# Two first expert slots computed together, and a routing table read three units later

## The chip, the cores and the metric

The kernel runs on one core of one Trainium2 chip. The metric is device time in microseconds (us): the median of three runs of one program, from its first to its last instruction and what lies around that. A profile is one further execution, recorded instruction by instruction. PE is the matrix engine (TensorE), DVE the vector engine, ACT the scalar engine, POOL is GpSimd, SP is the engine that issues most DMAs; PEld is the weight load that belongs to a matmul.

## What is computed

Three layers in a row, all in float32: causal attention with a cumulative bias (4 batches, 8 heads, 576 positions, 64 wide), a mixture of 8 experts over the 2304 tokens that leave it, and a gated layer.

```python
def _moe_ref(x, modality_id, w_gate, modality_bias, w1, w2) -> np.ndarray:
    logits = x @ w_gate + modality_bias[modality_id]
    e_idx = np.argmax(logits, axis=1)
    ...
    gate_w = probs[np.arange(N), e_idx]
    for e in range(E):
        mask = e_idx == e
        h = np.maximum(x[mask] @ w1[e], 0.0)
        out[mask] = gate_w[mask, None] * (h @ w2[e])

def _moe2_ref(x, w_gate, w_val, w_out) -> np.ndarray:
    gate = 1.0 / (1.0 + np.exp(-(x @ w_gate)))
    val = x @ w_val
    return (gate * val @ w_out).astype(np.float32)
```

Every token goes to one expert, the one with the largest logit. Which tokens an expert has is known only while the kernel runs. The change touches the passage from attention to the experts.

## The kernel before

**Attention** (`Attention.run`) works through 16 pairs of heads in an order written out by hand. A batch is done after four pairs. `Router.batch` then appends that batch's routing steps to a queue `router.q`; `tick()` issues one step between two attention instructions, `pump(n)` issues n at once.

**Routing of a batch.** DVE reduces the logits, finds each token's expert and makes a one-hot matrix `oh`. Six small matmuls on PE (tile `rp`, the rank product) turn it into each token's place among the tokens of its expert. DVE makes the address `r_ix`; POOL then writes the token numbers into a table `tab` in device memory with five indirect DMAs ("scatters", `tab<-ids,r_ix`) of up to 128 numbers each, and SP writes the batch's tokens to `x` (`x<-xr`, `rows_out`: one DMA of 1026 KB and one of 128 KB).

**Early slots.** Experts work in slots of 256 tokens. After two of the four batches the kernel guesses the expert with the most tokens (`on_guess`, which loads its weights into the `raw` tiles) and fills slots 0 and 1 with tokens of it. These two (`EARLY = 2`) run while batches 2 and 3 are still being routed. Slots 2 to 8 come after the whole table is known.

**A unit.** A slot is worked off in 8 units, one for each 128 columns of the hidden layer: 12 matmuls of the first product (`mm1`, tile `ph`), then 12 of the second product of the unit before (`mm2`, into `sb` for even slots and `y` for odd ones). Between the two products ACT makes the rounded hidden tile `hH`, and DVE its remainder `hL`. The weights are split likewise (`split`): for each of the two weight pieces of a unit a rounded copy (ACT) and a remainder (DVE), tiles `ew` for the early slots and `w` later. The first three splits are made by POOL alone. Slots 0 and 1 have the same weights, and each makes its own splits: slot 0 takes units 0 to 7, slot 1 units 8 to 15. A slot's tokens are scaled (`gate`, tile `xg`), transposed on PE (`mtr`, four 128x128 blocks at a time, two times) and split into `xT` by ACT and DVE before its first unit.

**From the table to slot 2.** In `early`, `main(u)` pumps 14 routing steps after each unit: what is left of batch 3, then the 60-odd small DVE steps of `Router.slots` that compute which slot has which expert. In the middle of these POOL reads the table rows of all slots back (`fetch_rows`, `tid<-tab,row`); it waits for every scatter. `indices` transposes them on PE (`itr<-ident,tid`) and DVE makes the row numbers `idx`, with which POOL gathers slot 2's tokens. Then all engines load the register `more` (are there rare slots?), and SP loads slot 2's weights over the `raw` tiles. PE takes its instructions in order, so what stands behind `itr` waits with it.

A finished slot is copied to `yt` and stored to `x2`.

Of the kernel before, what the change touches and what calls it, by code (L numbers as in the profile page):

```python
# [8 lines left out]
F32 = mybir.dt.float32  # L9
# [488 lines left out]
BIG = 100000.0  # L498
TROWS, PUMP = 96, 14
GAP, SP = [1, 1, 0, 0], [6, 3, 6, 0]  # L500
EARLY, EARLYB, MAIN, SLOTS, FIRST = 2, 2, 9, 14, 3
MAINH, HALVES, HROW, NROW = 2, 8, 32, 40


class Router:
    def __init__(self, tc, cp, ap, ps, ident, mod_bias, mod_id, x, tab, B, S):
        self.tc, self.nc = tc, tc.nc
        nc = self.nc
# [45 lines left out]
        self.gap, self.apart_of = 1, {"tab": [], "y": [], "out": []}  # L554
        self.q, self.hold, self.side = [], False, None

# [51 lines left out]
    def batch(self, b, xr, lg):  # L608
# [5 lines left out]
        tile_ = lambda shape, nm, dt=F32: cp.tile(shape, dt, tag="r_" + nm, name="r_" + nm)  # L614
        st = {}
        self.q.append(lambda: setattr(self, "gap", GAP[b]))
        bc = lambda a: a.unsqueeze(2).to_broadcast([128, 5, 8])
# [7 lines left out]
        q = self.q  # L625
# [40 lines left out]
        q.append(lambda: V.tensor_scalar(se, se, 1e-9, None, ALU.add))  # L666
        q.append(lambda: V.reciprocal(xr[:, :, 512], se))
        for t in range(5):
            rows = 64 if t == 4 else 128
            self.space(SP[b])  # L670
            q.append(lambda t=t, rows=rows: self.apart("tab", nc.gpsimd.indirect_dma_start(
                out=self.tab.rearrange("r c -> (r c)").unsqueeze(1),
                out_offset=bass.IndirectOffsetOnAxis(ap=ix[:rows, t : t + 1], axis=0),
                in_=self.ids[:rows, b, t : t + 1], in_offset=None, bounds_check=TROWS * 256 - 1, oob_is_err=True)))
            if t > 2:
                q.append(lambda t=t: self.rows_out(b, t, xr))
        if b == EARLYB - 1:
# [22 lines left out]
            q.append(lambda: V.tensor_copy(self.guess_i, gf[0:1]))  # L700
            q.append(self.on_guess)

    def rows_out(self, b, t, xr):

        x = self.x[2 * self.S * (b // 2) : 2 * self.S * (b // 2 + 1), :].rearrange("(p j) r -> p j r", j=XS)
        if t == 4:
            dst, src = x[64 * (b % 2) : 64 * (b % 2) + 64, 8, :], xr[:64, 4, :]  # L710
        else:
            dst, src = x[:, 4 * (b % 2) : 4 * (b % 2) + 4, :], xr[:, 0:4, :]
        self.nc.sync.dma_start(dst, src)

    def fetch_rows(self, tid, row, n):
        self.behind("tab", self.nc.gpsimd.indirect_dma_start(
            out=tid[:n, :], out_offset=None, in_=self.tab[:, :],
            in_offset=bass.IndirectOffsetOnAxis(ap=row[:n, 0:1], axis=0), bounds_check=TROWS - 1, oob_is_err=True,
        ))

    def indices(self, nm, tid, n, last):
# [24 lines left out]
    def slots(self):  # L746
# [79 lines left out]
        op(V.scalar_tensor_tensor, out=more, in0=inc[0:1, 8:9], scalar=float(MAIN), in1=s0[0:1], op0=ALU.is_gt, op1=ALU.max)  # L826
        q.append(lambda: self.indices("idx", self.tid, NROW, self.B * self.S - 1))
        op(V.tensor_copy, rg[:, 2:3], base)
# [53 lines left out]
class Moe:  # L882
# [8 lines left out]
    def open(self, ctx, early):  # L891
        P = lambda n, c: c.enter_context(self.tc.tile_pool(name=n, bufs=1, side="right", reuse_waits="tile"))
        self.wk, self.pe = P("m_work", ctx), P("m_early", early)
        self.xg_t = [self.wk.tile([128, 2, RW], F32, name=f"xg{i}") for i in range(3)]
        self.yt = self.wk.tile([128, 4, 256], F32, name="yt")

# [118 lines left out]
    def store(self, s):  # L1015

        nc, n = self.nc, 128 if s >= HROW else 256
        del self.xg[s]
        y = self.y.pop(s)
        for c, p in enumerate(y):  # L1020
            nc.scalar.copy(self.yt[:, 4 // len(y) * c : 4 // len(y) * (c + 1), :n], p.rearrange("p (a t) -> p a t", t=n))
        at = 256 * s if s < EARLY else self.base(s)
        nc.sync.dma_start(self.x2.rearrange("(c p) t -> p c t", p=128)[:, :, bass.ds(at, n)], self.yt[:, :, :n])
        if s >= EARLY:
            self.place(s, at, n)
# [6 lines left out]

    def mm(self, s, f):
        h = self.mm1(s, f)
        if self.prev:
            self.mm2(*self.prev)
        self.prev = (s, f, h)
# [88 lines left out]

    LE, LA = 2, 3

# [12 lines left out]
    def first(self):  # L1141
        for s in range(EARLY):
            self.gather(s)
        for f in range(self.LE + 1):
            self.split(0, f, self.nc.gpsimd)
            if f == 0:
                self.gate(0)
        self.v, self.u = self.LE + 1, 0

    def look(self):  # L1150
        for h in range(2):
            self.transpose(0, h)

    def step(self, u):
        s, f = divmod(u, 8)
        self.mm(s, f)
        if f == 3 and s >= EARLY and s + 2 < MAIN + MAINH:
            self.gather(s + 2 if s + 2 < MAIN else s + 2 - MAIN + HROW)
        if f == 1 and s + 1 < MAIN and s + 1 != EARLY:
            self.gate(s + 1)  # L1160
        if f == 4 and s + 1 == EARLY:
            self.gate(EARLY, True)
        if f in (4, 5) and s + 1 < MAIN:
            self.transpose(s + 1, f - 4)

    def next(self):
        self.step(self.u)
        self.u += 1
# [6 lines left out]
    def early(self, main):  # L1175

        for u in range(8 * EARLY):
            if u == self.u:
                self.next()
            while not self.ready:  # L1180
                self.ready = main(u)
                if u < 8 * EARLY - 5:
                    break
            self.loads()
            for s in range(EARLY, EARLY + 2):
                if self.ready and s not in self.xg and u >= 8 * (EARLY - 2) + 13 * (s - EARLY):
                    self.gather(s)
            self.aheads(self.LE if self.v < 8 * EARLY else self.LA)

# [534 lines left out]
def kernel(ctx, tc, q, k, v, s, modality_id, moe_w_gate, modality_bias, w1, w2, wg, wv, wo, out):  # L1724
    nc = tc.nc
# [9 lines left out]
    with tc.manual_schedule():  # L1735
# [47 lines left out]
        def main(u):  # L1783
            if u >= 0:
                router.pump(PUMP)
            if not router.q and phase[0] == 0:
# [5 lines left out]
            if router.q or not phase[0]:  # L1792
                return False
            for s in range(EARLY):
                moe.place(s, 256 * s)
            more.append(nc.values_load(router.more[0:1, 0:1], min_val=0, max_val=1))
            return True
# [6 lines left out]
        def put(at, tasks):  # L1804
            todo.setdefault(at, []).extend(tasks)
# [5 lines left out]
        for k, stages in enumerate(glu.last_weight(pool(wo_ctx, "dec", side="right", reuse_waits="tile"))):  # L1811
            for i, task in enumerate(stages):
                put(2 * k + i - 55, [task])
        put(-28, [wo_ctx.close, open_xs, glu.dec.load, glu.dec.load])
        (d0, s0), (d1, s1) = glu.w_tasks(0, lambda: xs[0]), glu.w_tasks(1)
# [84 lines left out]
```

## Time and profile before

| | us |
|---|---|
| median of three runs | 946.76 (944.15 to 948.65) |
| profiled execution, its own time | 945.87 |
| its span, first to last instruction | 944.1 |
| PE busy in it | 899.6 (95%) |
| DVE, ACT, POOL busy | 710.0, 554.1, 397.2 |
| units 0 to 15 (the two early slots), start of the first to end of the last | 59.96 |

The kernel is bound by PE nearly everywhere. In the span's 40 slices PE is below 90% in four: the first, the last, and those from 283 to 307 us and from 519 to 543 us. The granted clock of PE is below 90% in the first and in the one from 283 to 307 us; the latter lies in the early slots. Rows give start and length in us from the span's start; a bracket at the end is the time that the engine sat idle before the row and what ended it.

### The profile page before, as it was taken

Reading aid. Unit: us, or ns where it says so; the run is one execution under the profiler, and the core shown is the slowest. Engines: PE = TensorE matmul, PEld = TensorE weight load, DVE = VectorE, ACT = ScalarE, POOL = GpSimd, SP = SyncE. Lnnn points to the kernel's source line nnn. Section 1 sums busy time; section 2 is a strip of 40 time slices with the busy share of each in tenths; the row PEclk is TensorE's granted clock in tenths of the full one; section 3 lists DMA queues with packets and bytes.
Section 4 is the critical chain, followed back from the end, with each engine's and each line's share of the span. In section 5 each row is a group of like instructions: output and inputs, shape, how many; then the busy total and the mean of one; then the engine's idle time right before and its main releaser. Section 6 shows DMA issues by size and latency. Waiting matters only on the chain. (4 is left out here: it accounts for less than half of the span.)

```text
span 944.1 us, 18712 instructions
## 1 busy us (share of the span) xinstructions
PE 899.6 (95%) x6261; PEld 861.0 (91%) x6261; DVE 710.0 (75%) x1583; ACT 554.1 (59%) x1296; POOL 397.2 (42%) x616
## 2 busy tenths in 40 slices
PE   7999999999997999999999899999999999999996
PEld 6899889888887999999998799999999999889996
DVE  6999999999894688867766667767575747878771
ACT  4999899898643665656544455454545344454440
POOL 7988789798742577776630001010000000111111
PEclk8999999999998999999999999999999999999999
DMA  7667559694382355723467322333232308473501
GB/s 173 157 155 161 135 87 128 165 125 145 139 102 69 95 174 180 280 90 90 137 225 242 99 79 95 112 101 120 70 132 76 126 11 296 137 242 111 168 35 44
DMA packets 163903, 125.34 MB, mean 133 GB/s; under 512 B 86737, under 2 KB 147692, under 8 KB 163286
## 3 DMA queue, kind: packets, MB, share of 16 engines
q1 hardware_dynamic: 158790, 113.62, 44.5%
q0 software_dynamic: 3792, 10.14, 3.2%
q8 instruction: 51, 0.84, 0.4%
q14 instruction: 54, 0.44, 0.2%
q10 hardware_dynamic: 1216, 0.30, 0.1%
HBM read 115.95 MB, written 33.23 MB: 158 GB/s over the span
## 5 line engine op out<-in xcount | busy, mean ns | idle before, releaser
L1342 PE MATMUL X<-a,set 128*128 128x384 f32 x864 | 164.7, 338 | 4.8 <-ACTq L1072 3.0
L1342 PEld LDWEIGHTS X<-a,set 128*128 128x128 f32 x864 | 152.4, 188 | 6.6 <-ACTq L1072 3.1
L861 POOL TENSOR_SCALAR dn<-dr 128x256 int8<-128x256 int8 (+1 forms) x60 | 35.2, 588 | 251.3 <-DMA dr<-in_moe_w_gate_dram 96.6
L925 POOL TENSOR_TENSOR w<-raw,w 128x512 fp32r<-128x512 f32 x56 | 79.6, 1431 | 57.2 <-ACT w L922 54.7
L174 POOL TENSOR_SCALAR bias<-cumB,cumT 128x576 f32<-128x576 f32 (+4 forms) x155 | 82.6, 535 | 25.7 <-DVE nm L293 21.3
L1479 POOL DMA_INDIRECT out_dram<-oy,row x18 | 20.0, 1113 | 169.2 <-ACT oy L1503 92.0
L989 PE MATMUL ph<-xT,w 128*128 128x256 f32 x672 | 90.0, 283 | 0.0
L989 PEld LDWEIGHTS ph<-xT,w 128*128 128x128 f32 x672 | 83.6, 188 | 0.0
L1342 PE MATMUL Y<-a,set 128*128 128x384 f32 x432 | 82.0, 338 | 0.0
L302 ACT ACTIVATE P<-P,nm 128x576 f32<-128x576 f32 (+3 forms) x128 | 79.5, 627 | 3.3 <-DVE nm L293 3.2
L337 DVE TENSOR_TENSOR PL<-pt,PH 128x512 fp32r<-128x512 f32 (+1 forms) x128 | 77.0, 629 | 1.9 <-ACT PH L330 1.4
L1342 PEld LDWEIGHTS Y<-a,set 128*128 128x128 f32 x432 | 76.5, 188 | 0.1
L1351 ACT COPY u<-X 128x384 f32<-128x384 f32 x72 | 34.5, 479 | 62.8 <-PE X L1342 62.7
L293 DVE CUSTOM_DVE_ANT_0 P<-sb,bias 128x320 f32<-128x320 f32 (+3 forms) x128 | 67.1, 548 | 2.4 <-PE sb L284 1.9
L330 ACT CAST PH<-pt 128x512 fp32r<-128x512 f32 (+1 forms) x128 | 64.8, 552 | 6.8 <-PE pt L321 5.2
L321 PE MATMUL pt<-ident,P 128*128 128x128 f32 x448 | 64.2, 277 | 3.1 <-DVE PL L337 1.2
L925 DVE TENSOR_TENSOR w<-raw,w 128x512 fp32r<-128x512 f32 x56 | 57.0, 1019 | 11.6 <-ACT w L922 10.8
L922 ACT CAST w<-raw 128x512 fp32r<-128x512 f32 x112 | 63.5, 619 | 0.0
L993 ACT ACTIVATE hH<-ph 128x256 fp32r<-128x256 f32 x72 | 27.7, 384 | 59.7 <-PE ph L989 59.5
L284 PE MATMUL sb<-KT,QH 128*128 128x288 f32 (+3 forms) x192 | 56.3, 317 | 6.6 <-DVE nm L293 4.7
L321 PEld LDWEIGHTS pt<-ident,P 128*128 128x128 f32 x448 | 50.6, 141 | 9.6 <-DVE PL L337 1.9
L1277 ACT CAST hf<-hp 128x768 fp32r<-128x768 f32 x42 | 34.1, 835 | 38.5 <-DVE hp L1279 35.4
(317 smaller groups left out, 2430.9 us busy)
## 6 DMA issues: line engine op xcount, KB each, us to landing
raw<-in_moe_w_dram SPq DMA_DIRECT2D x80, 512.0 KB
h<-sg SPq DMA_DIRECT2D x72, 192.0 KB
cumB<-cum_d SPq DMA_DIRECT2D x32, 288.0 KB
hp<-h SPq DMA_DIRECT2D x24, 384.0 KB
qraw<-in_q_dram SPq DMA_DIRECT2D x58, 128.0 KB
dr<-in_moe_w_out_dram SPq DMA_DIRECT2D x12, 511.6 KB
dr<-in_moe_w_gate_dram SPq DMA_DIRECT2D x24, 255.2 KB
dr<-in_moe_w_val_dram SPq DMA_DIRECT2D x24, 255.2 KB
```

The source lines that it names most:

```text
L174: (nc.vector if n in FILLB else nc.gpsimd).tensor_scalar(res[i][:rows], cumB[:rows, :m], -1.0, self.cumT[:rows, i, n : n + 1], ALU.mult, A ...
L284: nc.tensor.matmul(self.sb[:rows, o : o + c1 - c0], X[:, T0[i] : T0[i] + rows], h["KT"][:, c0:c1], start=j == 0, stop=j == 1)
L293: nc.vector.tensor_tensor_reduce(out=pt[:rows, :m], in0=self.sb[:rows, o : o + m], in1=self.bias_t[n][i][:rows], op0=ALU.add, op1=ALU.min, ...
L302: nc.scalar.activation(h["P"][i][:rows, : T0[i] + rows], h["P"][i][:rows, : T0[i] + rows], AF.Exp, bias=h["nm", i][:rows], scale=-1.0, acc ...
L321: nc.tensor.transpose(pt[:, c : c + 128], h["P"][i][:, T0[j] : T0[j] + 128], self.ident)
L330: self.nc.scalar.copy(t[:, :z], pt[:, :z])
L337: self.nc.vector.tensor_tensor(t[:, :z], pt[:, :z], h["H"][u][:, :z].bitcast(F32), ALU.subtract)
L861: nc.gpsimd.tensor_scalar(o["n"], top(), 56.0, -56.0, ALU.min, ALU.max)
L922: nc.scalar.copy(v, src)
L925: (eng or nc.vector).tensor_tensor(v, src, h.bitcast(F32), ALU.subtract)
L989: nc.tensor.matmul(ph, w[:, 128 * dc : 128 * dc + 128], x[:, dc], start=k == 0, stop=k == 11)
L1342: self.nc.tensor.matmul(bank, w[:, c], a[:, h, c], start=first and k == 0, stop=k == 5, skip_group_check=True)
```

## The change

Slots 0 and 1 are run alternately: unit u is column block u // 2 of slot u % 2, and the block is split once for both. Slot 1's tokens are scaled and transposed before its first unit, now unit 1; slot 2's are transposed inside units 14 and 15, between the first and the second product.

The steps of `main` are spread differently: 9 steps after unit 0, none after units 1 and 2, and 14 after each unit from 3 on. The product `itr` moves from behind unit 7 to behind unit 10. The last batch's token rows go out on POOL's queue after its five scatters, no longer on SP's ahead of them. `on_guess` moves from the end of batch 1's steps to the start of batch 2's, and batch 2's scatters are held back until POOL has its first two splits behind it. Slot 2's weights can be loaded once slot 0 has used a block. The register `more` is loaded behind unit 36. `yt` has two buffers.

```diff
-TROWS, PUMP = 96, 14
-GAP, SP = [1, 1, 0, 0], [6, 3, 6, 0]
-EARLY, EARLYB, MAIN, SLOTS, FIRST = 2, 2, 9, 14, 3
+TROWS, PUMPS = 96, (9, 0, 0, 14)
+GAP, SP = [1, 1, 0, 0], [6, 3, 0, 0]
+EARLY, EARLYB, MAIN, SLOTS, IDX = 2, 2, 9, 14, 10
...
+        if b == EARLYB:
+            self.q.append(self.on_guess)
...
+        if b == EARLYB:
+            q.append(lambda: setattr(self, "hold", not self.started))
...
-            if t > 2:
-                q.append(lambda t=t: self.rows_out(b, t, xr))
+            if t > 2 and b < self.B - 1:
+                q.append(lambda t=t: self.rows_out(b, t, xr, nc.sync))
+        if b == self.B - 1:
+            for t in (3, 4):
+                q.append(lambda t=t: self.rows_out(b, t, xr, nc.gpsimd))
...
+    def numbers(self):
+        self.indices("idx", self.tid, NROW, self.B * self.S - 1)
...
+        yt = self.wk.tile([128, 4, 256], F32, tag="yt", name="yt", bufs=2)
...
     def first(self):
         for s in range(EARLY):
             self.gather(s)
-        for f in range(self.LE + 1):
+        for f in range(2):
             self.split(0, f, self.nc.gpsimd)
             if f == 0:
-                self.gate(0)
-        self.v, self.u = self.LE + 1, 0
+                for s in range(EARLY):
+                    self.gate(s)
+        self.r.hold, self.r.started = False, True
+        self.e, self.u, self.v = 2, 0, 8 * EARLY
+        self.pend.append((EARLY, 0))
...
+    def both(self, u):
+        f, s = divmod(u, EARLY)
+        self.shared = self.piece[s, f] = self.shared if s else self.piece[s, f]
+        left = 8 * EARLY - u
+        self.mm(s, f, (lambda: self.transpose(EARLY, 2 - left)) if left < 3 else None)
+        if left == 4:
+            self.gate(EARLY, True)
...
     def early(self, main):
+        for h in range(2):
+            self.transpose(1, h)
         for u in range(8 * EARLY):
             if u == self.u:
                 self.next()
             while not self.ready:
                 self.ready = main(u)
-                if u < 8 * EARLY - 5:
+                if u < IDX:
                     break
+            if u == IDX:
+                self.r.numbers()
+                for s in range(EARLY):
+                    self.place(s, 256 * s)
+                self.gather(EARLY)
+            if u == 8 * EARLY - 3:
+                self.gather(EARLY + 1)
+            while self.e < min(8, u // EARLY + 3):
+                self.split(0, self.e)
+                if self.e % 2 == 1:
+                    self.pend.append((EARLY, self.e // 2))
+                self.e += 1
             self.loads()
...
-                router.pump(PUMP)
+                router.pump(PUMPS[min(u, 3)])
...
-            more.append(nc.values_load(router.more[0:1, 0:1], min_val=0, max_val=1))
...
+        put(-36, [lambda: more.append(nc.values_load(router.more[0:1, 0:1], min_val=0, max_val=1))])
```

On PE, behind unit 0: `trx` and `ptx` are the last attention products, `ph` the first product of unit 1, `mtr` the transposes. Before:

```order
L381 MATMUL trx<-wgx,oT 128x144 x3
L381 MATMUL ptx<-wgx,oT 128x144 x2
L989 MATMUL ph<-xT_5178,ew 128x256
L989 MATMUL ph<-xT_5179,ew 128x256
L989 MATMUL ph<-xT_5178,ew 128x256 x2
```

Now:

```order
L381 MATMUL trx<-wgx,oT 128x144 x3
L381 MATMUL ptx<-wgx,oT 128x144 x2
L980 MATMUL mtr<-ident,xg_5066 128x128 x8
L996 MATMUL ph<-xT_5261,ew 128x256
L996 MATMUL ph<-xT_5262,ew 128x256
L996 MATMUL ph<-xT_5261,ew 128x256 x2
```

Slot 1's eight transposes (`xg_5066`) now stand directly ahead of slot 1's first unit, with nothing between them.

On DVE, the last batch's way from its logits to the one-hot matrix `oh_193`, which the rank product reads. Before:

```order
L626 TENSOR_REDUCE r_L<-lg_195 128x40
L627 TENSOR_TENSOR r_L<-r_L,tb 128x40
L628 TENSOR_REDUCE r_mx<-r_L 128x5
L629 TENSOR_TENSOR r_eq<-r_L,r_mx 128x40
L630 SCALAR_TENSOR_TENSOR r_eq<-r_eq,iota 128x40
L631 TENSOR_REDUCE r_em<-r_eq 128x5
L994 SCALAR_TENSOR_TENSOR hL<-ph,hH 128x256
L632 TENSOR_TENSOR oh_193<-iotax,r_em 128x40
```

Now:

```order
L932 TENSOR_TENSOR ew<-raw_1_84,ew 128x512
L1001 SCALAR_TENSOR_TENSOR hL<-ph,hH 128x256
L629 TENSOR_TENSOR r_L<-r_L,tb 128x40
L630 TENSOR_REDUCE r_mx<-r_L 128x5
L631 TENSOR_TENSOR r_eq<-r_L,r_mx 128x40
L632 SCALAR_TENSOR_TENSOR r_eq<-r_eq,iota 128x40
L633 TENSOR_REDUCE r_em<-r_eq 128x5
L634 TENSOR_TENSOR oh_193<-iotax,r_em 128x40
```

The six steps now stand behind the `hL` of unit 3; before, they ran during unit 1.

On POOL, from the scatters of batch 2 (`r_ix_4578`) to the gather of slot 2. Before:

```order
L671 DMA tab<-ids,r_ix_4578 24576x1 x5
L962 TENSOR_SCALAR xg_5066<-xg_5066 128x512 x2
L671 DMA tab<-ids,r_ix_5265 24576x1 x5
L716 DMA tid<-tab,row 40x256
L1796 TENSOR_LOAD more
L949 DMA xg_5067<-x,idx 128x513 x2
```

Now:

```order
L675 DMA tab<-ids,r_ix_4578 24576x1 x5
L675 DMA tab<-ids,r_ix_5258 24576x1 x5
L719 DMA x<-xr_197 128x2052
L719 DMA x<-xr_197 64x513
L722 DMA tid<-tab,row 40x256
L956 DMA xg_5067<-x,idx 128x513 x2
```

The scaling of slot 1 has left the place between the scatters, two DMAs with the last batch's token rows stand ahead of the read of the table, and the register load is gone from here.

## Rows read from the trace of the kernel before

**Rows 1.** Busy time by stretch: length, busy time (instructions) by engine, PEclk, DMA share, GB/s.

```profile
256.18:316.14 59.96, 52.09 (x410) 50.77 (x408) 42.65 (x144) 26.91 (x57) 20.64 (x19) 0.94 0.41 68
...
289.10:294.90 5.80, 5.54 (x26) 5.42 (x27) 2.02 (x5) 0.38 (x1) 3.37 (x4) 0.50 0.28 77
```

**Rows 2.** Timeline of PE: start, length, line, operation, tile, count, idle time before.

```profile
256.18 1.68 PE L989 MATMUL ph<-xT,ew 128*128 128x256 f32 x12
...
259.06 1.21 PE L989 MATMUL ph<-xT,ew 128*128 128x256 f32 x8
...
262.47 1.68 PE L989 MATMUL ph<-xT,ew 128*128 128x256 f32 x12
...
289.10 0.43 PE L725 MATMUL itr<-ident,tid 40*128 40x40 f32 x2 [6.28 <-DMA tid<-tab,row]
...
316.14 1.58 PE L989 MATMUL ph<-xT,w 128*128 128x256 f32 x12
...
330.37 0.60 PE L973 MATMUL mtr<-ident,xg 128*128 128x128 f32 x4
330.73 1.68 PE L989 MATMUL ph<-xT,w 128*128 128x256 f32 x12
```

**Rows 3.** PE's waits in 256 to 316.2 us: total, times, longest.

```profile
PE itr L725 <- DMA tid<-tab,row: 6.3, 1, 6.3
PE ph L989 <- DVE ew L925: 1.2, 2, 0.7
```

**Rows 4.** Groups by line and shape, 256.1 to 316.2 us: count, busy us, mean ns.

```profile
L925 DVE TENSOR_TENSOR ew<-raw,ew 128x512 fp32r<-128x512 f32 x26 | 17.2, 701 | 3.8 <-ACT ew L922 3.3 <-issue 0.3
L994 DVE SCALAR_TENSOR_TENSOR hL<-ph,hH 128x256 fp32r<-128x256 f32 x16 | 6.7, 417 | 4.1 <-ACT hH L993 4.1
L993 ACT ACTIVATE hH<-ph 128x256 fp32r<-128x256 f32 x16 | 6.2, 385 | 20.9 <-PE ph L989 20.9
...
L979 DVE TENSOR_TENSOR xT<-mtr,xT 128x512 fp32r<-128x512 f32 x4 | 2.8, 688 | 2.6 <-ACT xT L978 2.6
...
L978 ACT CAST xT<-mtr 128x512 fp32r<-128x512 f32 x4 | 2.3, 587 | 5.3 <-PE mtr L973 5.3
```

**Rows 5.** Timeline of POOL: batch 2's first scatter, scaling, last scatter, table read.

```profile
258.26 1.10 POOL L671 DMA_INDIRECT tab<-ids,r_ix  x1 [3.21 <-DVE r_ix L664]
...
264.49 2.38 POOL L962 TENSOR_SCALAR xg<-xg 128x512 f32<-128x512 f32 x2
...
274.08 0.91 POOL L671 DMA_INDIRECT tab<-ids,r_ix  x1 [1.61 <-DMA tab<-ids,r_ix]
286.54 1.03 POOL L716 DMA_INDIRECT tid<-tab,row  x1 [11.55 <-DMA tab<-ids,r_ix]
```

**Rows 6.** Issue to landing: ten scatters here, five in 130 to 165 us (medians), table reads.

```profile
tab<-ids,r_ix POOLq DMA_INDIRECT x10, 14.2
...
tab<-ids,r_ix POOLq DMA_INDIRECT x5, 9.1
...
DMA to landing us min/median/max: 2.3/2.3/2.3
```

**Rows 7.** SP's timeline, the four token-row DMAs; then a stretch as in rows 1.

```profile
259.73 5.99 SPq L713 DMA_DIRECT2D x<-xr  x4
...
282.00:287.00 5.00, 0.82 (x7) 0.62 (x6) 2.33 (x12) 1.14 (x2) 0.46 (x1) 1.00 0.00 0
```

**Rows 8.** Timeline of DVE: behind the rank product; first and 41st step of `slots`.

```profile
262.65 0.21 DVE L636 TENSOR_TENSOR r_R<-rp,cnt 128x48 f32<-128x48 f32 x1 [0.28 <-PE rp L641]
...
263.77 0.17 DVE L664 TENSOR_SCALAR r_ix<-r_rk 128x5 uint32<-128x5 f32 x1
...
268.27 0.22 DVE L765 TENSOR_TENSOR fill<-cnt,k 128x72 f32<-128x72 f32 x1
...
279.12 0.16 DVE L765 TENSOR_SCALAR sB<-nt 128x9 f32<-128x9 f32 x1
```

**Rows 9.** The load of the register `more` on PE: shortest, median, longest ns.

```profile
L1796 PEldq TENSOR_LOAD <-more x1: 483/483/483, 289.1 to 289.1; - x1
```

## What was predicted, and how

> **What bounds the kernel now.** PE is busy 95% of the span, so I looked for the place where it is not: the 40 slices show one inner stretch that loses both busy share and clock, 283 to 307 us, inside the early slots. The windows give the measure: units 0 to 15 last 59.96 us, with PE busy for 52.09 [rows 1]. What a unit costs undisturbed is read behind the stretch: five units of slot 2 start to start, (330.37 - 316.14) / 5 = 2.85 us [rows 2]. Sixteen of them are 45.6 us, so 14.4 us of the stretch are something else.
>
> PE's waits name the largest piece: 6.3 us at `itr`, for the table rows `tid` [rows 3]. The timeline shows it at 289.10, behind unit 7 [rows 2]. Behind the wait PE runs at half clock: in 289.10 to 294.90 the granted clock is 0.50, 1.2 of 2.4 GHz, with PE busy 5.54 us of 5.80 [rows 1]. Work that is half as fast costs half of that, about 2.8 us. The next piece is 1.2 us for DVE's `ew` [rows 3]. The rest is 16 transposes (four take 330.73 - 330.37 = 0.36 us start to start [rows 2], so 1.44), `itr` itself 0.4, and some 2.3 of small drags in units in which DVE has splits and routing steps together.
>
> Why is `tid` late? POOL issued the last scatter at 274.08, waited 11.55 us for the scatters to land, and issued the read at 286.54; the read lands 2.3 us after its issue [rows 5, 6]. From the last scatter to `itr` it is 15.0 us. In 282 to 287 the DMA share is 0.00 [rows 7]: what was outstanding was small.
>
> **Part 1, the wait at `itr` (removes 6.3 + 2.8).** PE's new schedule first. Everything ahead of 256.18 stays. Unit 0 ends at 259.06 [rows 2]. Then slot 1's eight transposes, 0.72, to 259.78, with nothing between them and unit 1. ACT rounds the two halves, 0.59 each, and DVE takes 0.69 behind the second [rows 4]: 259.42 + 2 x 0.59 + 0.69 = 261.3. The first product of unit 1 takes half a unit, 1.43, and would end at 261.2; its last half-dozen products need that remainder, so it ends near 262.3. **Wait here 1.1.** Second product: 263.75. Units 2 and 3: 269.45.
>
> Now the rank product, behind unit 3. Its six DVE steps stand behind unit 3's `hL`. That is ready 0.39 (ACT) and 0.42 (DVE) [rows 4] after the first product's end at 268.0, so at 268.85. The steps take 1.4 (from `r_R` to `r_ix`, a run of like steps, 262.65 to 263.94 [rows 8]). PE has the second product until 269.45 as cover and waits to 270.4: **wait 0.95**, product 0.15. Unit 4 begins at 270.55 and unit 11 would at 270.55 + 7 x 2.85 = 290.5, if `itr` behind unit 10 need not wait.
>
> Will `tid` be there? Address `r_ix` 1.5 us behind the rank product [rows 8], 271.9; first scatter 272.2; the fifth, at 1.3 each (0.91 to 1.10 plus 0.30 of issue [rows 5]) and without slot 1's scaling of 2.38 between, 277.4. The landing of scatters is not seen for this order; rows bound it: 2.3 us (the table read), 9.1 (five scatters of an earlier batch), 14.2 (ten together) [rows 6]. I take 9.1, since five now follow the other five late. Then 277.4 + 9.1 = 286.5, read and landing 2.56 (289.10 - 286.54) [rows 2, 5]: 289.1, so **no wait**, and the clock, which fell behind the idle 6.28 before [rows 2], stays. With 14.2 it is 294.2, a wait of 3.7; with the old 15.0 from last scatter to `itr`, 292.4, a wait of 1.9. These are ends of the range. The row address of the read comes from DVE in unit 7, about 282, and isn't last.
>
> **Part 2, shared splits.** `ew` on DVE falls from 26 to 12 at 0.70 us [rows 4], 9.8 us less of 50.77 busy, and as many rounded copies fewer on ACT. The 1.2 us wait and the drag go, if DVE isn't filled from elsewhere. It is, in units 5 to 8: 55 routing steps come there. The 41 steps from 268.27 to 279.28 took 11.0 us less two pairs of `ew`, two `hL`, two `xT` (2.80 + 0.83 + 1.38) [rows 4, 8], so 6.0, 0.147 each. 55 x 0.147 + 4 x 0.42 + 4 x 0.70 = 12.6 us against four units, 11.4. The 1.2 over are taken out of the slack of `hL`: it is ready 0.8 after the first product and needed only after the second of the unit before and the next unit's first, some 2 us later. **Cost 0**; bounds 0 and 1.2.
>
> **Part 3, slot 2.** Index numbers and the gather now come behind unit 10, at 290.85 (with 0.35 for `itr`). Before, the gathers were issued from 290.6, three quarters of a unit behind `itr`; now slot 2's transposes stand in units 14 and 15, 290.85 + 3 x 2.85 + 1.43 = 300.8 at the earliest. Four gathers at 1.3 and a landing of 2.3 (table read) give 299 with scaling of 2.4; 9.1 would make 303 and some 2 us of wait. Their queue is then empty of scatters, so I take the near one. The first transposes lie behind a first product, with a second as cover for `xT`. Cost beyond the 0.72 of PE time: 0. Weights of slot 2 are loaded two blocks earlier than before; two result buffers take a copy's wait for the store off ACT. Both 0, since PE never waits there now [rows 3].
>
> **Part 4, the register.** One load holds PE 0.48 us [rows 9]. Before, it stood at `itr`, at 289.1, behind the wait. At unit 36 it breaks into a full PE: 0.3 to 0.5; I take **0.5**.
>
> **The sum.** Unit 11 at 290.85, five units and slot 2's transposes: 290.85 + 14.25 + 0.72 = 305.8. Before: 316.14. Gain 10.3, less 0.5, is 9.8. The profiled execution of before took 945.87, 0.9 below the median of 946.76; from the profile that is 936.1, from the median 946.76 - 9.8 = **937.0**.
>
> **Rivals.**
> *A: the table is late again.* The wait goes from behind unit 7 to behind unit 10 and only shrinks: 1.9 to 3.7 us, 939 to 940.7, and with a clock drop of 2.8 behind it up to 943.5. For it: latency was 15.0 after ten scatters. Against it: three units (8.55 us) more of cover and a last scatter only 3.3 us later.
>
> *B, slower: the token rows clog POOL's queue.* The last batch's rows, 1.15 MB, went out on SP, at 259.73 to 265.7 [rows 7]; now POOL's queue has them between the scatters and the read of the table, in one queue. If they drain as slowly as the old mix of two batches' rows and ten scatters (259.73 to the read's issue at 286.54, 26.8 us [rows 5, 7]), then from 279.5 they end at 306.3, `tid` is there at 308.9, PE waits 18.4 and loses 2.4 more to the clock: 957.8. It turns slower than before from a wait of about 7.5 (`tid` at 298), where the gain of 9.8 is eaten with the clock. Against it: much of that old time was ten scatters on one path, and 282 to 287 moved nothing [rows 7].
> The Trainium skill, "DMA: Bandwidth & Descriptors", section "Two DMAs through the same engine are not ordered", says that within one queue of one engine descriptors start in order, which speaks against this change; no row shows POOL's queue with such rows in it. The same page's section on the anatomy of a DMA on the gpsimd path gives about 2.0 us plus bytes at 436 GB/s, by which 1.15 MB are an estimated 4.7 us, `tid` is in time and the sum stays.
>
> *C: DVE and the two new bare places are dearer.* Waits of 1.1 and 0.95 double, the 1.2 of part 2 and the 2 of part 3 come in: 937.0 + 2.05 + 1.2 + 2 = 942.2. For it: units 3 to 8 have less slack on DVE than before.
>
> *D: it doesn't do what it says,* since PE is as late elsewhere: `itr` in time, but slot 2 waits for its tokens at unit 14 for what was saved. Slot 2's gather also waits for the token rows, which now go out last. To eat 9.8 it must be some 12 us late; no row points there.
>
> **How the numbers follow.** About 0.5%, 4.7 us, is what a measurement of this kernel can tell from no change: faster is below 942.0, slower above 951.5. The forecast with its small bounds (934 to 939) has 0.55; A 0.22, nearly all of it below 942; C 0.15, half of it beyond 942; B 0.06, most of it slower; D 0.02. Faster 0.82, same 0.13, slower 0.05. The lower end takes in the waits of 1.1 and 0.95 at nothing and the register at 0.3: 934.7, and one more for the profile against the median. The upper end takes in A: 942.
>
> **What would show it.** On PE: `itr` behind unit 10 with a short wait or none, and a granted clock of 1.00 from 283 to 307; slot 2's first unit near 305.8; 1.1 us idle in unit 1 for `xT` and 0.95 at the rank product for `oh`. On POOL: last scatter near 277.4, table read at 282 to 287. On DVE: 12 `ew` in place of 26, and no wait of PE for `hL` in units 5 to 9. Wrong would be a long wait at `itr` (A, B), idle time at unit 14 (D), or PE behind DVE (C).

## The result and the profile after

The changed kernel takes 938.31 us (median of 4 runs, 936.73 to 939.85) against 946.0 us (4 runs); the ratio is 0.9916, 95% interval 0.9896 to 0.9936. Two later comparisons of the same two kernels, on two chips, gave 0.9896 (0.9859 to 0.9932) and 0.9910 (0.9889 to 0.9932). The gain is 7.7, 9.9 and 8.3 us by the medians; 9.8 was forecast.

| profiled execution, us | before | after |
|---|---|---|
| its own time | 945.87 | 939.85 |
| span | 944.1 | 938.1 |
| unit 0 to slot 2's first unit | 59.96 | 50.59 |
| PE idle at `itr` | 6.28 | 0 |
| granted clock of PE in 283 to 307 us | 0.86 | 1.00 |

First the stretch that the forecast was about, by windows (columns as in [rows 1]); the second window is where the kernel before had its hole.

```profile
257.34:307.93 50.59, 49.24 (x409) 48.36 (x408) 32.45 (x129) 18.55 (x39) 19.43 (x19) 1.00 0.42 70
...
283.00:307.00 24.00, 24.00 (x202) 23.81 (x201) 12.54 (x49) 9.03 (x19) 8.08 (x7) 1.00 0.39 76
```

PE is busy in 49.24 of 50.59 us, where it was busy in 52.09 of 59.96 [rows 1]. It does the same work in less busy time, since none of it is done at half clock. PE's waits in 256 to 312 us, which answer to [rows 3]:

```profile
PE rp L641 <- DVE oh L634: 0.8, 1, 0.8
PE ph L996 <- DVE xT L986: 0.3, 1, 0.3
PE ph L996 <- ACT xT L985: 0.2, 1, 0.2
```

`itr` is gone from the list, and so is `ew`; the new entries are the two bare places that the prediction named, with 0.6 us in place of 1.1 in unit 1 and 0.8 in place of 0.95 at the rank product. PE's timeline, which answers to [rows 2]:

```profile
257.34 1.69 PE L996 MATMUL ph<-xT,ew 128*128 128x256 f32 x12
...
260.30 1.04 PE L980 MATMUL mtr<-ident,xg 128*128 128x128 f32 x8
261.58 0.38 PE L996 MATMUL ph<-xT,ew 128*128 128x256 f32 x1 [0.24 <-ACT xT L985]
262.30 1.58 PE L996 MATMUL ph<-xT,ew 128*128 128x256 f32 x11 [0.34 <-DVE xT L986]
...
265.16 1.60 PE L996 MATMUL ph<-xT,ew 128*128 128x256 f32 x12
...
268.04 1.60 PE L996 MATMUL ph<-xT,ew 128*128 128x256 f32 x12
...
271.84 0.18 PE L641 MATMUL rp<-oh,tri 128*128 128x48 bf16 x1 [0.77 <-DVE oh L634]
271.87 0.27 PE L643 MATMUL rp<-oh,ones 128*128 128x40 bf16 x5
271.99 1.68 PE L996 MATMUL ph<-xT,ew 128*128 128x256 f32 x12
...
292.32 0.32 PE L734 MATMUL itr<-ident,tid 40*128 40x40 f32 x2
292.57 1.70 PE L996 MATMUL ph<-xT,ew 128*128 128x256 f32 x12
...
307.93 1.58 PE L996 MATMUL ph<-xT,w 128*128 128x256 f32 x12
```

`itr` has no bracket: PE did not wait. But it was close. POOL (columns as in [rows 5]) issued the read of the table 10.9 us behind the last scatter, and SP's next instruction that needs the rows, `ids<-tid`, went out at 292.31, when PE stood at `itr`:

```profile
278.85 0.91 POOL L675 DMA_INDIRECT tab<-ids,r_ix  x1 [0.30 <-issue]
279.76 1.21 POOL L719 DMA_DIRECT2D x<-xr  x2
289.75 1.07 POOL L722 DMA_INDIRECT tid<-tab,row  x1 [8.78 <-DVE rg L774]
```

The releaser in that last bracket is not to be believed: `rg` is the step of DVE that happened to end at that moment. The read needs `row`, which DVE had done by 284.6, and all scatters; in the next profile of the same program (`again`) it went out 1.8 us ahead of that step (287.64 and 289.40).

The stretch is 9.4 us shorter, the span only 6.0. Part of the rest lies where the change touches nothing. Windows of the changed kernel, same columns:

```profile
248.40:251.90 3.50, 3.50 (x13) 3.11 (x13) 1.40 (x3) 1.31 (x3) 3.33 (x4) 0.51 0.00 0
...
517.90:521.70 3.80, 3.78 (x13) 3.78 (x14) 0.00 (x0) 1.00 (x2) 0.00 (x0) 0.55 0.08 12
```

PE runs at half clock for 3.4 us in the last attention pairs and for as long at the start of the last layer; either would cost half of that, 1.7 us, if nothing hid it. The kernel before shows 1.00 in both places. Whether that belongs to the change was the first thing to find out.

### The profile page after: what moved, and what is told of

Same layout as the page of the kernel before. It is cut to its first block, busy times and chain, and to the rows that moved or that the text cites. A ratio compares the mean times of both kernels' runs of the same rounds, so it can differ in the third digit from the quotient of the medians.

```text
span 938.1 us, 18673 instructions
## 1 busy us (share of the span) xinstructions
PE 900.2 (96%) x6261; PEld 861.7 (92%) x6261; DVE 697.7 (74%) x1569; ACT 548.3 (58%) x1282; POOL 392.4 (42%) x614
## 5 line engine op out<-in xcount | busy, mean ns | idle before, releaser
L932 DVE TENSOR_TENSOR w<-raw,w 128x512 fp32r<-128x512 f32 x56 | 55.0, 982 | 12.2 <-ACT w L929 11.3
L360 PE MATMUL ot<-PH,vhl 128*128 128x512 f32 (+3 forms) x160 | 55.8, 359 | 1.1 <-DVE QL L258 1.0
```

The costliest lines, as they stand in the source:

```text
L932: (eng or nc.vector).tensor_tensor(v, src, h.bitcast(F32), ALU.subtract)
```

## The experiments

Each time stands beside the kernel before on the same chip. The stretch means the time from the start of unit 0 to the start of slot 2's first unit in the profile; it is 59.96 us before and 50.6 changed, and it repeats far better than whole times. The runs rows_sp, rank_unit1, reg_early and filled were timed on a chip on which the changed kernel was not; their ratios are set against its 0.9896 to 0.9916 on other chips.

**again: the changed kernel once more.** No edit.

> The changed kernel once more, unchanged, for a second profile and five more times. In its first profile PE ran at half clock for 3.3 us at 248 to 252 us, ahead of anything that the change moves, and again near 518 to 522 us; the kernel before had neither. Theory 1: these two dips come and go between executions. Then this profile lacks one or both of them, and its span is 1.0 to 2.7 us under 938.1 (935.4 to 937.1). Theory 2: they belong to the changed schedule. Then both stand in the same two places and the span is 938.1 within 0.5.

936.4 us against 946.27; ratio 0.9896 (0.9859 to 0.9932), span 935.5. Both half-clock pieces are missing:

```profile
257.11:307.71 50.60, 49.24 (x410) 48.36 (x408) 32.46 (x129) 18.55 (x39) 19.99 (x19) 1.00 0.43 70
248.00:252.00 4.00, 3.94 (x31) 3.45 (x32) 3.12 (x9) 2.39 (x8) 3.92 (x6) 1.00 0.00 0
517.00:522.00 5.00, 5.00 (x30) 4.84 (x29) 2.85 (x7) 2.28 (x6) 0.00 (x0) 1.00 0.42 122
```

Theory 1 holds: the drops come and go between executions of one program. The stretch is the same to 0.01 us. The span is 8.6 us under the kernel before's, against 6.0 in the first profile. The two pieces explain only a part of these 2.6 us: unit 0 begins 0.2 us earlier (257.11 for 257.34) and the last layer, from its first product `X`, is 0.9 us shorter; the other 1.4 us lie between slot 2's first unit and `X`, where the granted clock is 1.00 in both, and stay open.

**again2: and a third time,** beside the version "best" below.

> The changed kernel once more, beside the next one on the same chip. Its stretch was 50.6 us in two profiles, its ratio to the kernel before 0.990 and 0.992: I expect 0.990 within 0.003, the stretch 50.6, no wait at itr or one below 0.5 us.

937.53 against 945.79; ratio 0.9910 (0.9889 to 0.9932). The stretch is 50.75, with no wait recorded at `itr`, but SP got the rows at 291.98 and PE started `itr` at 291.96; the view of the tile `tid` has 0.3 us in which the weight load of `itr` waited for them. This profile has the drop near 518 and not the one near 250.

**idx7: the index product back behind unit 7.**

```diff
-EARLY, EARLYB, MAIN, SLOTS, IDX = 2, 2, 9, 14, 10
+EARLY, EARLYB, MAIN, SLOTS, IDX = 2, 2, 9, 14, 7
```

> The changed kernel with the index product itr behind unit 7 again, all else as changed. My theory (the wait for the table rows carried most of the gain): PE comes to itr near 284, the rows at 292.2 as before the move, so a wait of 8 us with a clock drop of 2 to 3 behind it, 10 to 11 us over the changed kernel: 948 to 949, about the kernel before or slower. Rival (shared splits carried it, the wait only moves work): 938 to 941.

949.28 against 946.27; ratio 1.0030 (1.0004 to 1.0057), with all other parts of the change in place. PE's row, and the windows of the wait and of what follows:

```profile
290.54 0.43 PE L734 MATMUL itr<-ident,tid 40*128 40x40 f32 x2 [7.47 <-DMA tid<-tab,row]
```

```profile
283.07:290.54 7.47, 0.00 (x1) 0.00 (x1) 3.70 (x31) 0.00 (x0) 1.07 (x1) 0.84 0.72 98
290.50:294.80 4.30, 4.26 (x20) 4.18 (x21) 0.68 (x3) 0.89 (x2) 2.14 (x3) 0.50 0.19 51
```

The stretch is 60.02: 50.6 + 7.47 + 2.15 for 4.3 us at half clock makes 60.2. Without the move of `itr` nothing of the gain is left.

**before_late: the kernel before with that one move.** `itr`, the gather and the register load wait until unit 10; slot 2's transposes go into units 14 and 15.

```diff
-            if router.q or not phase[0]:
+            if router.q or not phase[0] or u < 10:
                 return False
+            router.indices("idx", router.tid, NROW, router.B * router.S - 1)
...
-        self.mm(s, f)
+        self.mm(s, f, (lambda: self.transpose(EARLY, f - 6)) if s + 1 == EARLY and f > 5 else None)
```

> The kernel before with one edit: itr, the token gather and the register load behind unit 10 instead of 7, and slot 2's transposes in units 14 and 15. Own splits, slot after slot, scatters and token rows as before. My theory: the 6.3 us wait and the 2.8 us of half clock go, nothing else: 946.0 - 9.1 = 936.9, within 1.5, so as fast as the whole change or faster. Rival (the other parts were needed to bring the rows in time or to free DVE): a wait of some us remains at itr or at unit 14, 940 to 945.

940.89 against 946.27; ratio 0.9942 (0.9917 to 0.9966). The stretch is 51.39: 8.57 of the 9.37 us come from this move alone, and what is left over is PE waiting for DVE's splits, slightly more than before [rows 3]:

```profile
PE ph L988 <- DVE ew L924: 1.5, 3, 0.7
```

```profile
293.17 0.31 PE L725 MATMUL itr<-ident,tid 40*128 40x40 f32 x2
```

`itr` doesn't wait here, and it has room: SP's `ids<-tid`, which needs the table rows too, went out at 289.38, 3.8 us ahead of it, with the token rows on SP's queue as before. The changed kernel has no such room, since it also moves the last rank product, with all that follows from it, from unit 1 to unit 3.

The theory holds by the stretch and misses by the time: that is 4.5 us worse than the changed kernel's on the same chip, the stretch only 0.8. Its profile has a half-clock piece of 3.4 us at 518, 1.7 us of loss, and twice the loss of "again" in the first 24 us (3.4 against 1.7). The other runs point the same way: their mean granted clock is 0.9918 over ten runs here and 0.9945 over the six of "again". Where the clock is half, half of the time is lost; one less the mean clock, times a span of some 937 us, is then an estimated 7.7 us lost against 5.1. That is 2.6 of the 3.7 us between the two measures; why these runs had more of it, and the rest, stay open.

**own_splits: slot 1 makes its own splits again.**

```diff
...
-        self.shared = self.piece[s, f] = self.shared if s else self.piece[s, f]
...
-            while self.e < min(8, u // EARLY + 3):
-                self.split(0, self.e)
...
+            while self.e < min(16, u + 3):
+                f, s = divmod(self.e, EARLY)
+                self.split(s, f)
...
```

> The changed kernel in which slot 1 makes its own weight splits again; order of units, itr and the rest as changed. DVE gets 14 remainders of 0.68 us back, ACT 14 copies. My theory: in units 3 to 10 DVE is then behind PE, which waits 1.2 (as before) to 3.5 us (all that the stretch lost beside the itr wait): 939.5 to 942. Rival (the splits were hidden, sharing is worth nothing): 938.3 within 0.7. Rival (DVE is the bound once routing steps stand in the same units): over 3.5 us, 942 or more.

937.26 against the changed kernel's 936.4 in the same session; the ratios to before, 0.9909 (0.9876 to 0.9942) and 0.9896 (0.9859 to 0.9932), overlap. The stretch shows it: 52.09, 1.5 us more, all in units 7 to 10, where PE again waits for `ew`:

```profile
PE ph L996 <- DVE ew L932: 0.5, 2, 0.3
```

The rest of the 1.5 us is in pieces too short for that list. So sharing takes 9.6 us of work off DVE (32.45 us busy in the stretch in place of 42.03) and gives 1.5. My theory holds by the stretch (1.2 to 3.5 us), not by the time.

**rows_sp: the last batch's token rows back on SP's queue.**

```diff
-            if t > 2 and b < self.B - 1:
+            if t > 2:
                 q.append(lambda t=t: self.rows_out(b, t, xr, nc.sync))
-        if b == self.B - 1:
-            for t in (3, 4):
-                q.append(lambda t=t: self.rows_out(b, t, xr, nc.gpsimd))
```

> The changed kernel with the last batch's token rows on SP's queue ahead of its scatters again. The stretch from unit 0 to slot 2's first unit was 50.6 us in both profiles of the changed kernel, the read of the table was issued 9.0 and 10.9 us behind the last scatter. Theory B in small (the rows on POOL's queue hold the scatters or the read): the read comes 7 us or less behind the last scatter, the stretch stays 50.6 since the rows of the table were in time anyway. Rival (rows on SP are written among the scatters and slow them, as in the kernel before with 12.5 us): the read comes 11 to 13 us behind it, itr waits 0.5 to 2, the stretch is 51 to 52.5 and the time 1 to 2 us over the changed kernel's 937.

946.68 against 949.99; ratio 0.9964 (0.9946 to 0.9982). This one edit gives back most of the gain of 8 to 10 us. POOL's timeline, then PE's `itr`:

```profile
278.73 0.92 POOL L675 DMA_INDIRECT tab<-ids,r_ix  x1 [0.30 <-issue]
295.13 1.05 POOL L719 DMA_INDIRECT tid<-tab,row  x1 [15.48 <-DMA tab<-ids,r_ix]
```

```profile
297.74 0.43 PE L731 MATMUL itr<-ident,tid 40*128 40x40 f32 x2 [5.46 <-DMA tid<-tab,row]
```

The read comes 16.4 us behind the last scatter. Both theories fall, the one that the rows on POOL hold things up outright; the other had the direction, but 11 to 13 us. The stretch is 57.48: 50.6, the wait of 5.46, and 1.6 for the clock behind it.

**rows_behind: the token rows on POOL's queue, but behind the read of the table.**

```diff
-        if b == self.B - 1:
-            for t in (3, 4):
-                q.append(lambda t=t: self.rows_out(b, t, xr, nc.gpsimd))
...
         q.append(lambda: self.fetch_rows(self.tid, row, NROW))
+        for t in (3, 4):
+            q.append(lambda t=t: self.rows_out(self.B - 1, t, self.xr[(self.B - 1) % 2], nc.gpsimd))
```

> The changed kernel with the last batch's token rows on POOL's queue behind the read of the table instead of ahead of it. The read came 9.0 to 11.5 us behind the last scatter with the rows between. Theory (the rows delay the landing of the scatters): the read comes 6 to 8 us behind the last scatter and itr has 3 us of room. Rival (the scatters take that long by themselves): the read comes 9 to 11 us behind it again. In both the stretch is 50.6 unless slot 2's gather, which needs the rows, comes too late for units 14 and 15.

One run, 936.13. The read comes 8.2 us behind the last scatter (276.47 to 284.69), between the two forecasts, and the stretch is 50.60: the tokens came in time for units 14 and 15. With the 2.6 us from a read to its rows, `itr` at 289.95 has an estimated 2.7 us of room here. What the rows do to the scatters shows in the DMA view, one line per queue (packets, MB, share of 16 engines) and per issue (count, KB, median us from issue to landing). The changed kernel in 273 to 292 us:

```profile
q0 software_dynamic: 384, 1.23, 48.4%
...
tab<-ids,r_ix POOLq DMA_INDIRECT x5, 9.3
```

rows_sp in 272 to 296 us:

```profile
q1 hardware_dynamic: 224, 1.18, 41.6%
...
tab<-ids,r_ix POOLq DMA_INDIRECT x5, 16.5
```

rows_behind in 271 to 292 us:

```profile
q0 software_dynamic: 384, 1.23, 16.1%
...
x<-xr POOLq DMA_DIRECT2D x1, 1026.0 KB, 4.7
x<-xr POOLq DMA_DIRECT2D x1, 128.2 KB, 4.6
tab<-ids,r_ix POOLq DMA_INDIRECT x5, 7.4
```

Nearly the same bytes occupy the engines for 0.161 x 21 = 3.4 us when they go alone, 0.484 x 19 = 9.2 when they follow the scatters closely, and 0.416 x 24 = 10.0 when they go among them; the scatters land after 7.4, 9.3 and 16.5 us (medians of those whose landing the view has). Rows and scatters slow each other when they are under way together. How, no run here shows.

**rank_unit1: the last rank product behind unit 1 again.**

```diff
-TROWS, PUMPS = 96, (9, 0, 0, 14)
+TROWS, PUMPS = 96, (14, 14, 14, 14)
```

> The changed kernel with 14 routing steps after every unit from 0 on, so that the last rank product stands behind unit 1 again; splits shared, itr behind unit 10. My theory: the product's wait for oh stays (0.8 us, it only moves, since the steps are issued directly ahead of it), the table rows come 5.7 us earlier to an itr that waits for nothing, stretch 50.6 within 0.5, time the same. Rival (the late place was needed, because DVE has splits, transposes' remainders and steps in units 1 and 2): waits for ew or hL of 1 to 3 us in units 1 to 4, stretch 51.5 to 53.5.

941.87 against 949.99; ratio 0.9921 (0.9906 to 0.9936). The stretch is 50.90: the wait for `oh` only moves, 1.05 in place of 0.77, and the read of the table is issued 25 us into the stretch instead of 30.5 to 32.6, for an `itr` that has no use for it. No wait for `ew` or `hL` came up, so my theory holds but for one point: the table rows are here only some 4.6 us earlier, and not 5.7 (`ids<-tid` goes out 30.5 us into the stretch; in the two profiles of the changed kernel in which SP waited for the rows, 35.0 and 35.2).

The read itself took longer. POOL's timeline; SP's; SP's wait for the read; and the second DMA of the token rows in the DMA view:

```profile
281.38 1.21 POOL L719 DMA_DIRECT2D x<-xr  x2 [4.02 <-DVE sz L774]
283.86 1.60 POOL L722 DMA_INDIRECT tid<-tab,row  x1 [1.27 <-DVE s L774]
```

```profile
289.17 0.61 SPq L1039 DMA_DIRECT2D ids<-tid  x2
```

```profile
SPq L1039 <- DMA tid<-tab,row: 0.4, 1, 0.4
```

```profile
x<-xr POOLq DMA_DIRECT2D x1, 128.2 KB, 7.0
```

SP had its rows 5.3 us after the read's issue, where `itr` or SP had them 2.6 us after it in the changed kernel. The second of the two DMAs ahead of it, issued at 282.0, landed at 289.0. So this read, 2.5 us behind the token rows on the same queue, came back only when they had landed. The weight loads that SP issues at that time are not what held it: in the changed kernel they are issued around the read too (289.16 to 291.50), and it takes 2.6. In idx7, where it went out 8.3 us behind them, it took 3.2 us (287.38 to 290.54).

**reg_early: the register loaded behind `itr`, and one result buffer.** (`late` holds the load.)

```diff
+                self.r.numbers()
+                self.r.late()
...
-        put(-36, [lambda: more.append(nc.values_load(router.more[0:1, 0:1], min_val=0, max_val=1))])
...
-        yt = self.wk.tile([128, 4, 256], F32, tag="yt", name="yt", bufs=2)
+        yt = self.wk.tile([128, 4, 256], F32, tag="yt", name="yt", bufs=1)
```

> The changed kernel with the load of the register more directly behind itr (behind unit 10) in place of unit 36, and one result buffer yt in place of two. My theory: unit 36 gets 0.45 us shorter, unit 10 0.5 longer, so nothing in sum; with one yt ACT's copies at the end of slots wait, PE does not: time 937 within 1. Rival (the load is free behind itr, because the engines' sequencers have slack there): stretch stays 50.6, time 0.45 shorter. Rival (one yt matters): PE waits for y or hL at a slot's end, 1 us or more in all.

943.37 against 949.99; ratio 0.9932 (0.9916 to 0.9948), stretch 51.48. Of the 0.9 more, `tid` being late makes 0.54, and the load some 0.3. Unit 36 gave nothing back (3.61 us, with the load 3.60), so the load was free there.

The one buffer is the dearer half, and it shows behind the stretch. ACT's timeline, then PE's:

```profile
314.72 1.07 ACT L1029 COPY yt<-y 128x512 f32<-128x512 f32 x2 [3.76 <-DMA x<-yt]
```

```profile
317.17 0.38 PE L1016 MATMUL sb<-hH,w 128*128 128x256 f32 x1 [1.53 <-ACT hH L1000]
...
324.60 0.38 PE L1016 MATMUL sb<-hL,w 128*128 128x256 f32 x1 [1.01 <-DVE hL L1001]
```

Slots 0 and 1 now end one unit apart. ACT waits 3.76 us for slot 0's store before it can copy slot 1, slot 2's hidden tiles stand behind that copy, and PE waits for them. Two units of slot 2 take 4.98 and 4.48 us, where they take 2.85 and 3.21 with two buffers: 3.4 us more. The rival on `yt` was right. In the kernel before, the two copies lay 23 us apart (295.20 and 318.47) and one buffer was enough.

**filled: the two bare places covered.** Slot 1's transposes go ahead of `trx`; the steps to `oh` go behind unit 2, the rank product stays behind unit 3.

```diff
-TROWS, PUMPS = 96, (9, 0, 0, 14)
+TROWS, PUMPS = 96, (9, 0, 6, 14)
...
-    return {(2, "PVs", 0): free, (2, "PV", 1): moe.look, (1, "tx", 0): moe.next}
+    return {(2, "PVs", 0): free, (2, "PV", 1): moe.look, (1, "tx", 0): moe.start}
```

(`start` is `next` and the two transposes of slot 1.)

> The changed kernel with its two bare places covered: slot 1's eight transposes ahead of the last attention products (trx, ptx), and the six DVE steps to oh issued behind unit 2 instead of unit 3. My theory: the waits of 0.24 + 0.34 us in unit 1 and 0.77 at the rank product go, stretch 50.6 - 1.35 = 49.2 to 49.4, time 1.3 us under the changed kernel. Rival (the waits come back at the next place, ew or hL in units 2 and 3): stretch 50.0 or more.

938.62 against 949.99; ratio 0.9870 (0.9850 to 0.9890). The stretch is 50.13, not 49.3: the rival's size, at another place. Both waits are gone, but PE now reaches `itr` earlier than the rows do:

```profile
PE itr L734 <- DMA tid<-tab,row: 1.2, 1, 1.2
```

**idx9: `itr` one unit earlier than in the change.** `IDX` 9 in place of 10.

> The changed kernel with itr behind unit 9. The table rows came between 290.8 and 292.3, PE would come near 289.3: I expect a wait of 1.5 to 3.0 us at itr, one unit less than is needed. Theory: a wait this short leaves the granted clock at 1.00 behind it and the stretch is 52 to 53.5. Rival: the clock drops as it did behind 5.5, 6.3 and 7.5 us, and the stretch is 54 to 56.5.

One run, 943.81 against 945.79. The wait at `itr` is 2.69, in the range, and the rival on the clock is right; PE's row and the window behind it:

```profile
292.73 0.43 PE L734 MATMUL itr<-ident,tid 40*128 40x40 f32 x2 [2.69 <-DMA tid<-tab,row]
```

```profile
292.70:298.40 5.70, 5.67 (x27) 5.59 (x28) 1.36 (x3) 0.89 (x2) 3.24 (x4) 0.50 0.30 85
```

The stretch is 56.05: 50.6 + 2.69 + 2.8 for the clock. So unit 10 is the first place without a wait; the change has no unit to spare.

**best: filled, with the rank product a unit earlier.** The steps to `oh` stand behind unit 1 and the product behind unit 2; the register is loaded near the end, where PE waits for `hT`.

```diff
-TROWS, PUMPS = 96, (9, 0, 6, 14)
+TROWS, PUMPS = 96, (9, 6, 14, 14)
...
-        put(-36, [lambda: more.append(nc.values_load(router.more[0:1, 0:1], min_val=0, max_val=1))])
...
         self.hprev = None
+        self.r.late()
         self.half_mm2(*ready)
```

> The changed kernel with three places mended: slot 1's transposes ahead of trx and ptx; the six DVE steps to oh behind unit 1 and the rank product behind unit 2, one unit earlier, so that the table rows are 2.9 us earlier and the 1.25 us wait at itr that covering the bare places brought does not come; the register more loaded between the last half slot's transposes and its last product, where PE waits 1.1 us for hT. My theory: stretch 48.9 to 49.3, unit 36 shorter by 0.45, so 1.8 us under the changed kernel, ratio to it 0.998. Rival (a wait at itr or for ew comes back): stretch 50 or more, ratio 0.9995 to 1.001.

935.6 against 945.79, and 937.53 for the changed kernel in the same session; ratios to before 0.9887 (0.9863 to 0.9912) and 0.9910 (0.9889 to 0.9932). The intervals overlap, so the times alone don't separate the two; the stretch does, 48.80 against 50.75, with PE busy in 48.55 of it:

```profile
256.62:305.42 48.80, 48.55 (x409) 48.10 (x408) 32.15 (x129) 18.59 (x39) 19.50 (x19) 1.00 0.39 72
```

Here the read of `tid` was issued at 283.32, `itr` ran at 289.81, and no wait for it is left.

## Why the prediction was right, and where it was not

**The cause and the size.** The wait at `itr` and the half clock behind it were given 9.1 us. before_late, which removes only them, shortens the stretch by 8.57; idx7, which puts only them back, lengthens it by 9.4. That step was right. The whole times are less clear: before_late has 5.4 of the 9.9 us.

**PE's schedule.** Forecast for the stretch 49.6 (256.18 to 305.8), measured 50.59, 50.60 and 50.75. From slot 1's transposes to unit 2 it is 4.86 (260.30 to 265.16), forecast 4.69; unit 3 to unit 4 with the rank product 3.95 (268.04 to 271.99), forecast 3.95. The first agreement is in part luck, since the waits inside it were half of the forecast's. (For the six steps to `oh` the prediction took 1.4 us, where its rows, 262.65 to 263.94, give 1.29.) What was too small is the pace: units on `ew` tiles take 2.88 start to start, not slot 2's 2.85, as the prediction's own rows had it (256.18 to 259.06 [rows 2]), and slot 2's transposes inside a unit cost 0.44 for four and not 0.36 (301.30 to 304.62, less 2.88). Some 0.4 and 0.2 us; the rest of the 1.0 is 0.2 in unit 1 and small pieces.

**The landing of the scatters** was the weakest step. 9.1 us was taken and 1.4 us of room followed from it. The read was issued 10.9, 9.0 and 11.1 us behind the last scatter in three profiles of the changed kernel, later than the 282 to 287 us that the prediction named as a sign (289.75, 287.64, 289.41). So the rows came just in time, by luck of a unit's grid: in filled, where PE comes 1.7 us earlier, it waits 1.25, and in reg_early, whose edits stand behind `itr`, it waits 0.54. Rival A deserved more than 0.22 for a short wait.

**Rival B had the worse queue wrong.** It feared the token rows on POOL's queue, by the drain of the kernel before. They do delay the scatters there, by 1 to 3 us against rows_behind (8.2). But on SP's queue, where the change took them from, they delay them by 8. With the rank product as late as the change puts it, the part that the prediction treated as a risk is a condition of the gain; before_late keeps the product early and does without it. The Trainium skill ("DMA: Bandwidth & Descriptors", the section on the anatomy of a DMA on the gpsimd path) has a fit that gives an estimated 4.7 us for the 1026 and 128 KB as one transfer; rows_behind shows 4.7 and 4.6 for the two where they go alone, and the engines' 9.2 us against 3.4 show that it doesn't hold among the scatters (in "again" the 128 KB land 10.8 us after their issue).

The other half of B, a read held up by rows ahead of it in its queue, does occur: 5.3 us in rank_unit1, against 2.6. In the changed kernel it costs nothing, since the scatters hold the read back until the rows are nearly through: from its issue to `itr` it was 2.6 us (289.75 to 292.32), where a read took 2.3 before [rows 6]. Behind the read, as in rows_behind, the rows would be out of its way as well.

**Sharing the splits.** The prediction counted the 1.2 us wait and 2.3 of drag as gone with 14 remainders. own_splits gives 1.5 back. The work taken off DVE was mostly covered, so this step failed: it put all 3.5 us to the splits. That units 5 to 8 would bear 55 routing steps at no cost was right: they run at 2.88 each.

**Two result buffers** were put at 0, "since PE never waits there now". Against the kernel before that is right. But in the new order one buffer costs 3.4 us (reg_early), so the second is a condition of the gain, as the rows' queue is; the prediction had not seen that the two slots now end together.

**The register.** 0.5 was charged; it costs 0. The load runs for 0.50 us on PE's queue, at 371.5, inside unit 36, and the unit is as long as without it. The changed kernel's load, from the view of the tile `more`, and PE's timeline at the starts of units 36 and 37; then PE's timeline of the kernel before at the same two units:

```profile
L1843 PEldq TENSOR_LOAD <-more x1: 502/502/502, 371.5 to 371.5; - x1
```

```profile
369.32 1.58 PE L996 MATMUL ph<-xT,w 128*128 128x256 f32 x12
...
372.92 1.31 PE L996 MATMUL ph<-xT,w 128*128 128x256 f32 x9
```

```profile
377.46 1.59 PE L989 MATMUL ph<-xT,w 128*128 128x256 f32 x12
...
381.07 1.21 PE L989 MATMUL ph<-xT,w 128*128 128x256 f32 x8
```

3.60 and 3.61 us. The 0.5 too much and the 1.0 too little cancel in part: 9.4 from the trace, against 9.8.

**Ahead of the stretch** "everything stays" was right for the instructions and wrong for the clock time: unit 0 began between 254.95 and 260.20 us over 14 profiles, with half-clock pieces that came and went. They are not all of it: again and own_splits have the same 3.4 us of half clock ahead of unit 0 and differ by 2.0 us (257.11 and 255.11). A span can't carry a statement on 2 us here; the stretch can.

## What to carry to other kernels

When PE waits for a chain through device memory, move the consumer in PE's order until the chain is covered, and price the lost clock behind the wait with the wait itself: here they were 6.3 and 2.8 of 9.4 us. Then look at what else the same engines carry while the small transfers are out; where the bulk rows went was worth 7 us. When an order brings two results closer together, ask whether their buffers still come free in time; here that was worth 3.4 us. Leave more room than one profile says, since the time from the last scatter to the read varied by 2 us between executions of the same program.

## What the runs showed of the hardware

- The granted clock fell to 0.50 behind PE waits of 2.7 (idx9), 5.5 (rows_sp), 6.3 [rows 1, 2] and 7.5 us (idx7), and PE then worked at half clock for 3.2 (rows_sp) to 6.3 us (idx9). Behind 1.25 us (filled) it stayed at 1.00.
- Behind a wait of 2.7 to 3.0 us at the start of the last layer it fell in 9 of 14 profiles and not in the others; again and again2 are the same program and differ in it.
- 1.15 MB of rows and five scatters of up to 128 four-byte elements take 4.7 and 7.4 us apart (rows_behind); together, the scatters took 8.7 (idx9) to 16.5 us (rows_sp), depending on the queue and the moment at which the rows go out.
- A read of 40 table rows took 2.3 us [rows 6] to 2.6 us from issue to use, and 5.3 us in rank_unit1, 2.5 us behind 1.15 MB of rows on the same queue.
